# Loading wo, gate and up in whole transfers and projecting after all heads, in a one-token transformer block

## Chip, cores, metric

One NeuronCore of one Trainium2 chip. The metric is device time in microseconds (us); most executions agree within 0.3%. The span of a profile is about 2 us shorter than the time of a run.

## The reference

One token (S = 1, D = 640) goes through attention over the last W = 1024 positions of a K/V cache with 32 heads of 128, and a gated feed-forward part with F = 1728. Everything is bf16.

```python
h  = x + A(layernorm(x))      # q = x@wq; softmax(q k^T / sqrt(128)) v over the last 1024 positions; @wo
h2 = h + B(layernorm(h))      # (gelu(x@w_gate) * (x@w_up)) @ w_down
```

There is next to no reuse: 33.9 MB of cache and weights are read once. A *run* below is a stretch of bytes that lie together both in DRAM and in a partition of SBUF; a *packet* is one record of a DMA engine in the trace, and here a run is one packet.

## The kernel before

All loads are issued from one queue, in order: x, wq (2), K (16), V (8) with a quarter of wo behind every second V, gate and up in two column halves, wd (5). The parts that matter here:

```python
ones_f32 = const.tile([P, P], fp32, name="ones_f32")
one11_bf = const.tile([1, 1], bf16, name="one11_bf")
...
x_row = work.tile([1, D], bf16, name="x_row")
...
wo_src = A_wo.rearrange("(h d) n -> d h n", d=Dh)          # runs of 640 x 2 B
for c in range(NGV):
    vnat = vpool.tile([P, GV, NS, Dh], bf16, name="vnat")
    q.dma_start(out=vnat[...], in_=A_v_cache[...].rearrange("g (p t) d -> p g t d", t=NS))   # runs of 2048 B
    if c % 2 == 1:
        q.dma_start(out=wo_sb[:, woc*8:(woc+1)*8, :], in_=wo_src[:, woc*8:(woc+1)*8, :])
for (b0, b1) in cg_bounds:                                   # 2 column halves
    q.dma_start(out=wgu_sb[:, 0, :, c0:c1], in_=wg_src[:, :, c0:c1])
    q.dma_start(out=wgu_sb[:, 1, :, c0:c1], in_=wu_src[:, :, c0:c1])
...                                                          # wd in 5 transfers
for h in range(Hq):
    emit_pv(h)                                               # 8 matmuls and a cast
    if h % 8 == 4 and h // 8 >= 1:
        emit_oproj_group(h // 8 - 1)                         # 40 matmuls between V tiles
emit_oproj_group(3)
...                                                          # LayerNorm
for (b0, b1) in cg_bounds:                                   # gate and up of a half, gelu of that half
    ...
for kt in range(NFT):                                        # down: 70 matmuls
    ...
```

Of the kernel before, what the change touches and what calls it, by code (L numbers as in the profile page):

```python
# [9 lines left out]
ALU = mybir.AluOpType  # L10
ACT = mybir.ActivationFunctionType
AX = mybir.AxisListType
# [3 lines left out]
def kernel(  # L16
# [13 lines left out]
    nc = tc.nc  # L30
    bf16 = mybir.dt.bfloat16
    fp32 = mybir.dt.float32
    P = 128

    D = A_x.shape[-1]
    KT = D // P
    Dh = 128
    Hq = A_wq.shape[1] // Dh
# [6 lines left out]
    F = B_w_gate.shape[1]  # L45
    NFT = (F + P - 1) // P
# [9 lines left out]
    q = nc.sync  # L56

    const = ctx.enter_context(tc.tile_pool(name="const", bufs=1))
    wpool = ctx.enter_context(tc.tile_pool(name="wpool", bufs=1))
    work = ctx.enter_context(tc.tile_pool(name="work", bufs=1))  # L60
# [5 lines left out]
    ident_bf = const.tile([P, P], bf16, name="ident_bf")  # L66
    make_identity(nc, ident_bf[:])
    ones_f32 = const.tile([P, P], fp32, name="ones_f32")
    nc.vector.memset(ones_f32[:], 1.0)
    one11_bf = const.tile([1, 1], bf16, name="one11_bf")  # L70
    nc.vector.memset(one11_bf[:], 1.0)
    eps_t = const.tile([P, 1], fp32, name="eps_t")
    nc.vector.memset(eps_t[:], eps)

    x_row = work.tile([1, D], bf16, name="x_row")
    q.dma_start(out=x_row[:], in_=A_x.rearrange("b s d -> (b s) d"))  # L76

    wq_sb = wpool.tile([P, KT, Hq * Dh], bf16, name="wq_sb", tag="wA")
    wo_sb = wpool.tile([P, Hq, D], bf16, name="wo_sb", tag="wA")
    wgu_sb = wpool.tile([P, 2, KT, F], bf16, name="wgu_sb", tag="wF")  # L80
    wd_sb = wpool.tile([P, NFT, D], bf16, name="wd_sb", tag="wD")

# [6 lines left out]
    for c in range(NG):  # L89
        knat = kpool.tile([P, G, NS, Dh], bf16, name="knat")  # L90
        q.dma_start(  # L91
            out=knat[:, :, :, :],
            in_=A_k_cache[0, c * G : (c + 1) * G, S0:Sk, :].rearrange("g (p t) d -> p g t d", t=NS),
        )
        k_tiles.append(knat)
    wo_src = A_wo.rearrange("(h d) n -> d h n", d=Dh)
    WOCH = 8
    v_tiles = []
    for c in range(NGV):
        vnat = vpool.tile([P, GV, NS, Dh], bf16, name="vnat")  # L100
        q.dma_start(  # L101
            out=vnat[:, :, :, :],
            in_=A_v_cache[0, c * GV : (c + 1) * GV, S0:Sk, :].rearrange("g (p t) d -> p g t d", t=NS),
        )
        v_tiles.append(vnat)
        if c % 2 == 1:
            woc = c // 2
            q.dma_start(out=wo_sb[:, woc * WOCH : (woc + 1) * WOCH, :], in_=wo_src[:, woc * WOCH : (woc + 1) * WOCH, :])  # L108
    wg_src = B_w_gate.rearrange("(kt p) n -> p kt n", p=P)
    wu_src = B_w_up.rearrange("(kt p) n -> p kt n", p=P)  # L110
    NCG = 2
    cg_bounds = []
    b = 0
    for i in range(NCG):
        e = b + (NFT - b + (NCG - i) - 1) // (NCG - i)
        cg_bounds.append((b, e))
        b = e
    for (b0, b1) in cg_bounds:
        c0, c1 = b0 * P, min(b1 * P, F)
        q.dma_start(out=wgu_sb[:, 0, :, c0:c1], in_=wg_src[:, :, c0:c1])  # L120
        q.dma_start(out=wgu_sb[:, 1, :, c0:c1], in_=wu_src[:, :, c0:c1])  # L121
    nfull = NFT - 1
    wd_full_src = B_w_down[0 : nfull * P, :].rearrange("(kt p) n -> p kt n", p=P)
    NWD = 4
    b = 0
    for i in range(NWD):
        e = b + (nfull - b + (NWD - i) - 1) // (NWD - i)
        q.dma_start(out=wd_sb[:, b:e, :], in_=wd_full_src[:, b:e, :])  # L128
        b = e
# [3 lines left out]
    for c in range(KT):  # L133
        nc.tensor.matmul(
            xcol_ps[:, c : c + 1],
            lhsT=x_row[0:1, c * P : (c + 1) * P],
            rhs=one11_bf[0:1, 0:1],
            start=True,
            stop=True,
        )  # L140
    stats1 = work.tile([P, 2 * KT], fp32, name="stats1")
    nc.vector.tensor_copy(out=stats1[:, 0:KT], in_=xcol_ps[:, 0:KT])
    nc.vector.tensor_tensor(
        out=stats1[:, KT : 2 * KT], in0=stats1[:, 0:KT], in1=stats1[:, 0:KT], op=ALU.mult
# [7 lines left out]
    def ln_stats(bsum_ps, tagp):  # L152
# [24 lines left out]
        out=xn_col[:, :],  # L177
        in0=stats1[:, 0:KT],
        scalar1=mean1[:, 0:1],
        scalar2=rstd1[:, 0:1],  # L180
        op0=ALU.subtract,
        op1=ALU.mult,
# [4 lines left out]
    for h in range(Hq):  # L187
        for kt in range(KT):
            nc.tensor.matmul(  # L189
                q_ps[:, h : h + 1],  # L190
                lhsT=wq_sb[:, kt, h * Dh : (h + 1) * Dh],
                rhs=xn_col[:, kt : kt + 1],
                start=(kt == 0),
                stop=(kt == KT - 1),
# [48 lines left out]
    for t in range(NS):  # L243
        nc.tensor.transpose(
            out=srow_ps[0:Hq, t * P : (t + 1) * P],
            in_=sc_sb[:, t, :],
# [9 lines left out]
        out=e_sb[:, :],  # L256
        in_=srow_ps[0:Hq, :],
        func=ACT.Exp,
        bias=nbias[:, 0:1],
        scale=sm_scale,  # L260
# [7 lines left out]
    for t in range(NS):  # L268
        nc.tensor.transpose(
            out=eT_ps[:, t, :],  # L270
            in_=e_sb[0:Hq, t * P : (t + 1) * P],
# [7 lines left out]
    att2 = att2_ctx.enter_context(tc.tile_pool(name="att2", bufs=1, space=bass.MemoryType.PSUM))  # L279
    NOB = 4  # L280
    o_ps = att2.tile([P, NOB, 512], fp32, name="o_ps")
    o_sb = work.tile([P, Hq], bf16, name="o_sb")
    HG = 8
    NHG = Hq // HG
    opart_ps = att2.tile([P, NHG, KT], fp32, name="opart_ps")

    def emit_pv(h):
        vnat = v_tiles[(h // rep) // GV]
        g = (h // rep) % GV
        ocol = o_ps[:, h % NOB, (h // NOB) : (h // NOB) + 1]  # L290
        for t in range(NS):
            nc.tensor.matmul(  # L292
                ocol,
                lhsT=vnat[:, g, t, :],
                rhs=eT_sb[:, t, h : h + 1],
                start=(t == 0),
                stop=(t == NS - 1),
            )
        nc.vector.tensor_copy(out=o_sb[:, h : h + 1], in_=ocol)  # L299

    def emit_oproj_group(hg):
        for n in range(KT):
            for j in range(HG):
                h = hg * HG + j
                nc.tensor.matmul(  # L305
                    opart_ps[:, hg, n : n + 1],
                    lhsT=wo_sb[:, h, n * P : (n + 1) * P],
                    rhs=o_sb[:, h : h + 1],
                    start=(j == 0),
                    stop=(j == HG - 1),  # L310
                )

    for h in range(Hq):
        emit_pv(h)
        if h % HG == HG // 2 and h // HG >= 1:
            emit_oproj_group(h // HG - 1)
    emit_oproj_group(NHG - 1)
    attn_col = work.tile([P, KT], fp32, name="attn_col")
    nc.vector.tensor_reduce(
        out=attn_col[:, :],  # L320
        in_=opart_ps[:, :, :].rearrange("p g n -> p n g"),
        axis=AX.X,
        op=ALU.add,
    )

    h_col = work.tile([P, KT], fp32, name="h_col")
    nc.vector.tensor_tensor(out=h_col[:, :], in0=stats1[:, 0:KT], in1=attn_col[:, :], op=ALU.add)
    att2_ctx.close()
    stats2 = work.tile([P, 2 * KT], fp32, name="stats2")
    nc.vector.tensor_copy(out=stats2[:, 0:KT], in_=h_col[:, :])  # L330
# [3 lines left out]
    mean2, rstd2 = ln_stats(bsum2_ps, "ln2")  # L334
    hn_col = work.tile([P, KT], bf16, name="hn_col")
    nc.vector.tensor_scalar(
        out=hn_col[:, :], in0=h_col[:, :], scalar1=mean2[:, 0:1], scalar2=None, op0=ALU.subtract
# [3 lines left out]
    gu_ps = ffn_psum.tile([P, 2, NFT], fp32, name="gu_ps")  # L341
    nc.vector.memset(gu_ps[:, :, :], 0.0)
    down5 = ffn_psum.tile([P, KT, 512], fp32, name="down5")
    rsh = work.tile([P, 1], fp32, name="rsh")
    nc.vector.tensor_scalar_mul(out=rsh[:, :], in0=rstd2[:, 0:1], scalar1=0.5)
    g_sb = work.tile([P, NFT], fp32, name="g_sb")
    t1 = work.tile([P, NFT], fp32, name="t1")
    t2 = work.tile([P, NFT], fp32, name="t2")
    th = work.tile([P, NFT], fp32, name="th")
    gh = work.tile([P, NFT], fp32, name="gh")  # L350
    a_sb = work.tile([P, NFT], bf16, name="a_sb")
    for (b0, b1) in cg_bounds:
        for nt in range(b0, b1):
            M = P if nt < NFT - 1 else FT_LAST
            for which in range(2):
                for kt in range(KT):
                    nc.tensor.matmul(  # L357
                        gu_ps[0:M, which, nt : nt + 1],
                        lhsT=wgu_sb[:, which, kt, nt * P : nt * P + M],
                        rhs=hn_col[:, kt : kt + 1],  # L360
                        start=(kt == 0),
                        stop=(kt == KT - 1),
                    )
        sl = slice(b0, b1)
        nc.vector.tensor_scalar_mul(out=g_sb[:, sl], in0=gu_ps[:, 0, sl], scalar1=rstd2[:, 0:1])  # L365
        nc.vector.tensor_tensor(out=t1[:, sl], in0=g_sb[:, sl], in1=g_sb[:, sl], op=ALU.mult)
        nc.vector.tensor_scalar(
            out=t1[:, sl], in0=t1[:, sl], scalar1=0.044715, scalar2=1.0, op0=ALU.mult, op1=ALU.add
        )
        nc.vector.tensor_tensor(out=t2[:, sl], in0=t1[:, sl], in1=g_sb[:, sl], op=ALU.mult)  # L370
        nc.scalar.activation(out=th[:, sl], in_=t2[:, sl], func=ACT.Tanh, scale=0.7978845608028654)
        nc.vector.scalar_tensor_tensor(
            out=gh[:, sl], in0=th[:, sl], scalar=1.0, in1=g_sb[:, sl], op0=ALU.add, op1=ALU.mult
        )
        nc.vector.scalar_tensor_tensor(
            out=a_sb[:, sl], in0=gu_ps[:, 1, sl], scalar=rsh[:, 0:1], in1=gh[:, sl], op0=ALU.mult, op1=ALU.mult
        )
    for kt in range(NFT):
        K = P if kt < NFT - 1 else FT_LAST
        for n in range(KT):  # L380
            nc.tensor.matmul(  # L381
                down5[:, n, 0:1],
                lhsT=wd_sb[0:K, kt, n * P : (n + 1) * P],
# [41 lines left out]
```

## Time and profile before

| | before |
|---|---|
| time, median of the first 5 runs | 100.46 us (100.18 to 101.45) |
| span of the profile | 98.4 us |
| queue of loads, share of 16 engines | 94.7% |
| busiest compute engine (TensorE) | 58% |

The page, its row of slices and the stretches are read in the prediction below. Two further lines of the profile before: the first, from the page, counts the packets of the DMA engines. The second is the table of stretches for 18 to 34 us, where only K is loaded (start and end, length, busy time of the five engines, granted clock, DMA share, GB/s). The DMA share is the summed time of the packets over that of 16 engines; it can pass 1, because packets overlap a little.

```profile
DMA packets 18503, 34.08 MB, mean 346 GB/s; under 512 B 635, under 2 KB 9020, under 8 KB 18492
```

```profile
18.00:34.00 16.00, 15.36 (x335) 15.05 (x336) 7.42 (x12) 5.06 (x5) 0.00 (x0) 0.77 1.05 385
```

### The profile page before, as it was taken

The page shows a single profiled execution, that of the slowest core. Times are in us where ns is not written, and L with a number is a line of the kernel's source. Part 1 is how long each engine was busy: PE and PEld are TensorE (multiplying, and loading weights), DVE is VectorE, ACT ScalarE, POOL GpSimd, SP SyncE. Part 2 cuts the span into 40 slices and gives each one's busy share as a digit, 9 for nine tenths or more (in the row PEclk, how much of TensorE's full clock was granted, in tenths as well). Part 3 has the DMA queues.
Part 4 walks back from the last instruction along what each step waited for, and adds up shares of the span by engine and source line. Part 5 has one row for each costly group of instructions (what it writes and reads, how often), then busy time and mean ns, then how long its engine had stood idle before and what let it go on. Part 6 is the DMA issues. An engine that isn't in the chain of part 4 may idle for free.

```text
span 98.4 us, 3010 instructions
## 1 busy us (share of the span) xinstructions
PE 57.4 (58%) x1380; PEld 54.1 (55%) x1380; DVE 27.3 (28%) x95; ACT 18.9 (19%) x23; POOL 0.7 (1%) x6
## 2 busy tenths in 40 slices
PE   1791790699999999996129259044441511618650
PEld 0790790699989898985119259034331501618540
DVE  1310000035465556564535023020220320210400
ACT  5240000004436272544280000000000070000000
POOL 2000000000000000000000000000000000000000
PEclk9999855555899999999955555555555555555555
DMA  1899999999999999999999999999999999999400
GB/s 14 300 381 390 419 423 392 387 386 383 384 386 385 382 387 384 386 381 361 381 387 372 363 382 385 367 373 386 377 366 375 383 378 375 378 371 355 164 17 1
DMA packets 18503, 34.08 MB, mean 346 GB/s; under 512 B 635, under 2 KB 9020, under 8 KB 18492
## 3 DMA queue, kind: packets, MB, share of 16 engines
q1 hardware_dynamic: 18492, 33.90, 94.7%
q8 instruction: 10, 0.16, 0.7%
q14 instruction: 1, 0.01, 0.0%
HBM read 33.90 MB, written 0.00 MB: 344 GB/s over the span
## 4 chain that ended last, share of the span: by engine, by line
SPq 54%; DMA 27%; PE 14%; issue 1%; DVE 1%; DVEq 0%
SPq L101 23%; DMA wq_sb<-in_A_wq_dram 17%; DMA wd_sb<-in_B_w_down_dram 10%; SPq L108 9%; PE kT_ps L213 8%; SPq L120 7%; SPq L128 7%; SPq L121 7%; PE q_ps L189 2%; PE sc_ps L226 2%; PE down L381 1%; DVE kT_sb L218 1%; SPq L87 0%; SPq L91 0%; SPq L76 0%
## 5 line engine op out<-in xcount | busy, mean ns | idle before, releaser
L213 PE MATMUL kT_ps<-ident_bf,knat 128*128 128x128 bf16 x256 | 18.8, 234 | 0.0
L216 ACT COPY kT_sb<-kT_ps 128x1024 bf16<-128x1024 bf16 x11 | 11.1, 1012 | 28.5 <-PE kT_ps L213 28.5
L218 DVE COPY kT_sb<-kT_ps 128x1024 bf16<-128x1024 bf16 x21 | 13.7, 687 | 10.5 <-PE kT_ps L213 10.5
L213 PEld LDWEIGHTS <-knat 128*128 128x128 bf16 x256 | 16.4, 106 | 0.0
L292 PE MATMUL o_ps<-eT_sb,vnat 128*128 128x1 bf16 x256 | 7.9, 165 | 9.3 <-issue 5.6
L292 PEld LDWEIGHTS <-vnat 128*128 128x128 bf16 x256 | 7.4, 104 | 9.7 <-issue 6.3
L226 PE MATMUL sc_ps<-q_sb,kT_sb 128*128 128x1 bf16 x256 | 10.0, 164 | 1.4 <-DVE kT_sb L218 0.9
L226 PEld LDWEIGHTS <-kT_sb 128*128 128x128 bf16 x256 | 8.8, 97 | 2.1 <-DVE kT_sb L218 1.3
L299 DVE CAST o_sb<-o_ps 128x1 bf16<-128x1 f32 x32 | 5.2, 161 | 17.0 <-PE o_ps L292 15.7
L357 PE MATMUL gu_ps<-hn_col,wgu_sb 128*128 128x1 bf16 (+1 forms) x140 | 4.7, 168 | 8.1 <-DMA wgu_sb<-in_B_w_up_dram 4.6
L357 PEld LDWEIGHTS <-wgu_sb 128*128 128x128 bf16 (+1 forms) x140 | 4.5, 108 | 8.3 <-DMA wgu_sb<-in_B_w_up_dram 4.8
L189 PE MATMUL q_ps<-xn_col,wq_sb 128*128 128x1 bf16 x160 | 4.5, 165 | 6.1 <-DMA wq_sb<-in_A_wq_dram 6.1
L189 PEld LDWEIGHTS <-wq_sb 128*128 128x128 bf16 x160 | 4.3, 102 | 6.6 <-DMA wq_sb<-in_A_wq_dram 6.6
L305 PE MATMUL opart_ps<-o_sb,wo_sb 128*128 128x1 bf16 x160 | 5.2, 165 | 4.3 <-DMA wo_sb<-in_A_wo_dram 4.2
L305 PEld LDWEIGHTS <-wo_sb 128*128 128x128 bf16 x160 | 4.8, 104 | 4.6 <-DMA wo_sb<-in_A_wo_dram 4.4
L169 ACT ACTIVATE lnv_ln<-var_ln,eps_t 128x1 f32<-128x1 f32 x2 | 0.6, 294 | 30.3 <-DVE var_ln L165 30.3
L150 PEld LDWEIGHTS <-ident_bf 128*128 128x128 bf16 x36 | 4.0, 150 | 0.3 <-issue 0.3
L150 PE MATMUL junk_ps<-ident_bf 128*128 128x128 bf16 x36 | 4.0, 310 | 0.3 <-DVE tot_ln L154 0.3
L200 DVE CAST q_sb<-q_ps 128x32 bf16<-128x32 f32 x1 | 0.2, 192 | 14.1 <-PE q_ps L189 14.1
L381 PE MATMUL down<-a_sb,wd_sb 128*128 128x1 bf16 (+1 forms) x70 | 2.6, 166 | 1.7 <-DMA wd_sb<-in_B_w_down_dram 1.7
L381 PEld LDWEIGHTS <-wd_sb 128*128 128x128 bf16 (+1 forms) x70 | 2.3, 105 | 2.0 <-DMA wd_sb<-in_B_w_down_dram 2.0
L365 DVE TENSOR_SCALAR g_sb<-gu_ps,rstd_ln 128x7 f32<-128x7 f32 x2 | 0.5, 226 | 8.5 <-PE gu_ps L357 8.5
(56 smaller groups left out, 25.4 us busy)
## 6 DMA issues: line engine op xcount, KB each, us to landing
knat<-in_A_k_cache_dram SPq DMA_DIRECT2D x16, 512.0 KB, 10.8
vnat<-in_A_v_cache_dram SPq DMA_DIRECT2D x8, 1024.0 KB, 13.5
wq_sb<-in_A_wq_dram SPq DMA_DIRECT2D x2, 2560.0 KB, 13.0
wo_sb<-in_A_wo_dram SPq DMA_DIRECT2D x4, 1280.0 KB, 14.4
wd_sb<-in_B_w_down_dram SPq DMA_DIRECT2D x3, 480.0 KB, 10.3
wgu_sb<-in_B_w_gate_dram SPq DMA_DIRECT2D x1, 1120.0 KB, 16.8
wgu_sb<-in_B_w_up_dram SPq DMA_DIRECT2D x1, 1120.0 KB
wgu_sb<-in_B_w_gate_dram SPq DMA_DIRECT2D x1, 1040.0 KB, 15.4
```

The costliest lines, as they stand in the source:

```text
L101: q.dma_start(out=vnat[:, :, :, :], in_=A_v_cache[0, c * GV : (c + 1) * GV, S0:Sk, :].rearrange("g (p t) d -> p g t d", t=NS),)
L108: q.dma_start(out=wo_sb[:, woc * WOCH : (woc + 1) * WOCH, :], in_=wo_src[:, woc * WOCH : (woc + 1) * WOCH, :])
L120: q.dma_start(out=wgu_sb[:, 0, :, c0:c1], in_=wg_src[:, :, c0:c1])
L150: nc.tensor.matmul(junk_ps[:, :], lhsT=ident_bf[:, :], rhs=ident_bf[:, :], start=True, stop=True)
L189: nc.tensor.matmul(q_ps[:, h : h + 1], lhsT=wq_sb[:, kt, h * Dh : (h + 1) * Dh], rhs=xn_col[:, kt : kt + 1], start=(kt == 0), stop=(kt == ...
L213: nc.tensor.transpose(out=kT_ps[:, t, :], in_=knat[:, g, t, :], identity=ident_bf[:, :])
L216: nc.scalar.copy(out=kT_sb[:, :, :], in_=kT_ps[:, :, :])
L218: nc.vector.tensor_copy(out=kT_sb[:, :, :], in_=kT_ps[:, :, :])
L226: nc.tensor.matmul(sc_ps[:, t, h : h + 1], lhsT=kT_sb[:, t, :], rhs=q_sb[:, h : h + 1], start=True, stop=True,)
L292: nc.tensor.matmul(ocol, lhsT=vnat[:, g, t, :], rhs=eT_sb[:, t, h : h + 1], start=(t == 0), stop=(t == NS - 1),)
L305: nc.tensor.matmul(opart_ps[:, hg, n : n + 1], lhsT=wo_sb[:, h, n * P : (n + 1) * P], rhs=o_sb[:, h : h + 1], start=(j == 0), stop=(j == H ...
L357: nc.tensor.matmul(gu_ps[0:M, which, nt : nt + 1], lhsT=wgu_sb[:, which, kt, nt * P : nt * P + M], rhs=hn_col[:, kt : kt + 1], start=(kt = ...
```

## The change

The intent: fewer and longer runs in the loads, and one projection after all heads instead of four groups. wo is viewed so that a partition holds 32 neighbouring rows; o must then be permuted to match, which a 32x32 block transpose and a matmul with a permutation do.

```diff
+    perm_bf = const.tile([P, P], bf16, name="perm_bf")
+    nc.vector.tensor_copy(out=perm_bf ... "p (h a)", in_=ident_bf ... "p (a h)")
+    padc = const.tile([P, 32], bf16, name="padc")
+    nc.vector.memset(padc[:], 0.0)
...
+    pad = work.tile([P, 64], bf16, name="pad")
+    nc.vector.memset(pad[:], 0.0)
     x_row = work.tile([1, D], bf16, name="x_row")
...
-    wo_src = A_wo.rearrange("(h d) n -> d h n", d=Dh)
+    wo_src = A_wo.rearrange("(p r) n -> p (r n)", p=P)
+    q.dma_start(out=wo_sb[:, :, :].rearrange("p r n -> p (r n)"), in_=wo_src)     # ahead of V
     for c in range(NGV):
...
-        if c % 2 == 1:
-            q.dma_start(out=wo_sb[:, woc * WOCH : ...], in_=wo_src[...])
...
-    for (b0, b1) in cg_bounds:
-        q.dma_start(out=wgu_sb[:, 0, :, c0:c1], in_=wg_src[:, :, c0:c1])
-        q.dma_start(out=wgu_sb[:, 1, :, c0:c1], in_=wu_src[:, :, c0:c1])
+    q.dma_start(out=wgu_sb[:, 0, :, :], in_=wg_src[:, :, :])
+    q.dma_start(out=wgu_sb[:, 1, :, :], in_=wu_src[:, :, :])
...
-    (o projection in 4 groups of 40 matmuls between the heads, and a sum of the groups)
+    nc.vector.transpose(out=o_blk[:, :], in_=o_sb[:, :])
+    nc.tensor.matmul(perm_ps[:, :], lhsT=perm_bf[:, :], rhs=o_blk[:, :], start=True, stop=True)
+    nc.vector.tensor_copy(out=o_perm[:, :], in_=perm_ps[:, :])
+    (160 matmuls of wo_sb[:, r, ...] with o_perm[:, r])
...
-    (gate, up and gelu in two column halves)
+    (all of gate, all of up, then gelu once)
```

More of the change, by code (lines that the diff above doesn't have):

```diff
@@ L69 @@
     nc.vector.memset(ones_f32[:], 1.0)
+    perm_bf = const.tile([P, P], bf16, name="perm_bf")
+    nc.vector.tensor_copy(
+        out=perm_bf[:, :].rearrange("p (h a) -> p h a", a=4),
+        in_=ident_bf[:, :].rearrange("p (a h) -> p h a", a=4),
+    )
+    padc = const.tile([P, 32], bf16, name="padc")
+    nc.vector.memset(padc[:], 0.0)
     one11_bf = const.tile([1, 1], bf16, name="one11_bf")
@@ L78 @@
     wq_sb = wpool.tile([P, KT, Hq * Dh], bf16, name="wq_sb", tag="wA")
-    wo_sb = wpool.tile([P, Hq, D], bf16, name="wo_sb", tag="wA")
+    DJ = Dh // 32
+    RWO = (Hq * Dh) // P
+    wo_sb = wpool.tile([P, RWO, D], bf16, name="wo_sb", tag="wA")
     wgu_sb = wpool.tile([P, 2, KT, F], bf16, name="wgu_sb", tag="wF")
@@ L95 @@
         k_tiles.append(knat)
-    wo_src = A_wo.rearrange("(h d) n -> d h n", d=Dh)
-    WOCH = 8
+    wo_src = A_wo.rearrange("(p r) n -> p (r n)", p=P)
+    q.dma_start(out=wo_sb[:, :, :].rearrange("p r n -> p (r n)"), in_=wo_src)
     v_tiles = []
@@ L105 @@
         v_tiles.append(vnat)
-        if c % 2 == 1:
-            woc = c // 2
-            q.dma_start(out=wo_sb[:, woc * WOCH : (woc + 1) * WOCH, :], in_=wo_src[:, woc * WOCH : (woc + 1) * WOCH, :])
     wg_src = B_w_gate.rearrange("(kt p) n -> p kt n", p=P)
     wu_src = B_w_up.rearrange("(kt p) n -> p kt n", p=P)
-    NCG = 2
-    cg_bounds = []
-    b = 0
-    for i in range(NCG):
-        e = b + (NFT - b + (NCG - i) - 1) // (NCG - i)
-        cg_bounds.append((b, e))
-        b = e
-    for (b0, b1) in cg_bounds:
-        c0, c1 = b0 * P, min(b1 * P, F)
-        q.dma_start(out=wgu_sb[:, 0, :, c0:c1], in_=wg_src[:, :, c0:c1])
-        q.dma_start(out=wgu_sb[:, 1, :, c0:c1], in_=wu_src[:, :, c0:c1])
+    q.dma_start(out=wgu_sb[:, 0, :, :], in_=wg_src[:, :, :])
+    q.dma_start(out=wgu_sb[:, 1, :, :], in_=wu_src[:, :, :])
     nfull = NFT - 1
@@ L282 @@
     o_sb = work.tile([P, Hq], bf16, name="o_sb")
-    HG = 8
-    NHG = Hq // HG
-    opart_ps = att2.tile([P, NHG, KT], fp32, name="opart_ps")
-    def emit_pv(h):
+    for h in range(Hq):
         vnat = v_tiles[(h // rep) // GV]
@@ L299, in emit_pv @@
         nc.vector.tensor_copy(out=o_sb[:, h : h + 1], in_=ocol)
-    def emit_oproj_group(hg):
-        for n in range(KT):
-            for j in range(HG):
-                h = hg * HG + j
-                nc.tensor.matmul(
-                    opart_ps[:, hg, n : n + 1],
-                    lhsT=wo_sb[:, h, n * P : (n + 1) * P],
-                    rhs=o_sb[:, h : h + 1],
-                    start=(j == 0),
-                    stop=(j == HG - 1),
-                )
-    for h in range(Hq):
-        emit_pv(h)
-        if h % HG == HG // 2 and h // HG >= 1:
-            emit_oproj_group(h // HG - 1)
-    emit_oproj_group(NHG - 1)
-    attn_col = work.tile([P, KT], fp32, name="attn_col")
-    nc.vector.tensor_reduce(
-        out=attn_col[:, :],
-        in_=opart_ps[:, :, :].rearrange("p g n -> p n g"),
-        axis=AX.X,
-        op=ALU.add,
-    )
+    o_perm = work.tile([P, 32], bf16, name="o_perm")
+    o_blk = work.tile([P, 32], bf16, name="o_blk")
+    nc.vector.transpose(out=o_blk[:, :], in_=o_sb[:, :])
+    perm_ps = att2.tile([P, 32], fp32, name="perm_ps")
+    nc.tensor.matmul(
+        perm_ps[:, :],
+        lhsT=perm_bf[:, :],
+        rhs=o_blk[:, :],
+        start=True,
+        stop=True,
+    )
+    nc.vector.tensor_copy(out=o_perm[:, :], in_=perm_ps[:, :])
+    attn_ps = att2.tile([P, KT], fp32, name="attn_ps")
+    for n in range(KT):
+        for r in range(RWO):
+            nc.tensor.matmul(
+                attn_ps[:, n : n + 1],
+                lhsT=wo_sb[:, r, n * P : (n + 1) * P],
+                rhs=o_perm[:, r : r + 1],
+                start=(r == 0),
+                stop=(r == RWO - 1),
+            )
     h_col = work.tile([P, KT], fp32, name="h_col")
-    nc.vector.tensor_tensor(out=h_col[:, :], in0=stats1[:, 0:KT], in1=attn_col[:, :], op=ALU.add)
+    nc.vector.tensor_tensor(out=h_col[:, :], in0=stats1[:, 0:KT], in1=attn_ps[:, :], op=ALU.add)
     att2_ctx.close()
@@ L351 @@
     a_sb = work.tile([P, NFT], bf16, name="a_sb")
-    for (b0, b1) in cg_bounds:
-        for nt in range(b0, b1):
+    for which in range(2):
+        for nt in range(NFT):
             M = P if nt < NFT - 1 else FT_LAST
-            for which in range(2):
-                for kt in range(KT):
-                    nc.tensor.matmul(
-                        gu_ps[0:M, which, nt : nt + 1],
-                        lhsT=wgu_sb[:, which, kt, nt * P : nt * P + M],
-                        rhs=hn_col[:, kt : kt + 1],
-                        start=(kt == 0),
-                        stop=(kt == KT - 1),
-                    )
-        sl = slice(b0, b1)
-        nc.vector.tensor_scalar_mul(out=g_sb[:, sl], in0=gu_ps[:, 0, sl], scalar1=rstd2[:, 0:1])
-        nc.vector.tensor_tensor(out=t1[:, sl], in0=g_sb[:, sl], in1=g_sb[:, sl], op=ALU.mult)
-        nc.vector.tensor_scalar(
-            out=t1[:, sl], in0=t1[:, sl], scalar1=0.044715, scalar2=1.0, op0=ALU.mult, op1=ALU.add
-        )
-        nc.vector.tensor_tensor(out=t2[:, sl], in0=t1[:, sl], in1=g_sb[:, sl], op=ALU.mult)
-        nc.scalar.activation(out=th[:, sl], in_=t2[:, sl], func=ACT.Tanh, scale=0.7978845608028654)
-        nc.vector.scalar_tensor_tensor(
-            out=gh[:, sl], in0=th[:, sl], scalar=1.0, in1=g_sb[:, sl], op0=ALU.add, op1=ALU.mult
-        )
-        nc.vector.scalar_tensor_tensor(
-            out=a_sb[:, sl], in0=gu_ps[:, 1, sl], scalar=rsh[:, 0:1], in1=gh[:, sl], op0=ALU.mult, op1=ALU.mult
-        )
@@ new lines @@
+            for kt in range(KT):
+                nc.tensor.matmul(
+                    gu_ps[0:M, which, nt : nt + 1],
+                    lhsT=wgu_sb[:, which, kt, nt * P : nt * P + M],
+                    rhs=hn_col[:, kt : kt + 1],
+                    start=(kt == 0),
+                    stop=(kt == KT - 1),
+                )
+    sl = slice(0, NFT)
+    nc.vector.tensor_scalar_mul(out=g_sb[:, sl], in0=gu_ps[:, 0, sl], scalar1=rstd2[:, 0:1])
+    nc.vector.tensor_tensor(out=t1[:, sl], in0=g_sb[:, sl], in1=g_sb[:, sl], op=ALU.mult)
@@ new lines @@
+    nc.vector.tensor_scalar(
+        out=t1[:, sl], in0=t1[:, sl], scalar1=0.044715, scalar2=1.0, op0=ALU.mult, op1=ALU.add
+    )
+    nc.vector.tensor_tensor(out=t2[:, sl], in0=t1[:, sl], in1=g_sb[:, sl], op=ALU.mult)
+    nc.scalar.activation(out=th[:, sl], in_=t2[:, sl], func=ACT.Tanh, scale=0.7978845608028654)
+    nc.vector.scalar_tensor_tensor(
+        out=gh[:, sl], in0=th[:, sl], scalar=1.0, in1=g_sb[:, sl], op0=ALU.add, op1=ALU.mult
+    )
+    nc.vector.scalar_tensor_tensor(
+        out=a_sb[:, sl], in0=gu_ps[:, 1, sl], scalar=rsh[:, 0:1], in1=gh[:, sl], op0=ALU.mult, op1=ALU.mult
+    )
```

## The prediction

> **What bounds the kernel now.** I read the page from the top: busy shares, the row of slices, the chain that ended last, the transfers, then the timeline of the last 25 us and the table of stretches.
>
> The slices first. The three rows are the TensorE clock in tenths, the busy share of the DMA engines and their GB/s, 2.46 us to a digit:
>
> ```profile
> PE 57.4 (58%) x1380; PEld 54.1 (55%) x1380; DVE 27.3 (28%) x95; ACT 18.9 (19%) x23; POOL 0.7 (1%) x6
> ...
> PEclk9999855555899999999955555555555555555555
> DMA  1899999999999999999999999999999999999400
> GB/s 14 300 381 390 419 423 392 387 386 383 384 386 385 382 387 384 386 381 361 381 387 372 363 382 385 367 373 386 377 366 375 383 378 375 378 371 355 164 17 1
> ```
>
> No compute engine is busy over 58%, while the DMA row is at 9 from slice 2 to slice 36. So the kernel is one stream of 33.9 MB, and its end is the end of the stream plus what is computed after it. The chain agrees: it is made of the queue's issues[...] and of two transfers.
>
> ```profile
> SPq 54%; DMA 27%; PE 14%; issue 1%; DVE 1%; DVEq 0%
> ```
>
> The timeline of the end shows what stands behind the last byte:
>
> ```profile
> 94.72 0.70 PEld L381 LDWEIGHTS <-wd_sb 128*128 128x128 bf16 x20 [0.83 <-DMA wd_sb<-in_B_w_down_dram]
> 94.73 0.79 PE L381 MATMUL down<-a_sb,wd_sb 128*128 128x1 bf16 x20 [0.74 <-DMA wd_sb<-in_B_w_down_dram]
> ...
> 96.31 0.30 SPq L394 DMA_DIRECT2D out_dram<-outT_sb  x1
> ```
>
> The last piece of wd lands at 94.7 us; the other 3.7 us of the 98.4 us span are 20 matmuls, an add, a transpose, a copy and the store, which the change leaves alone.
>
> Last, the rate of the stream by stretch. In each row the last two numbers are the DMA share and GB/s. The stretches are wq alone, K, V mixed with wo, gate and up, and wd:
>
> ```profile
> 4.00:15.00 11.00, 8.07 (x135) 7.54 (x133) 0.48 (x3) 1.78 (x3) 0.00 (x0) 0.85 1.02 405
> 18.00:40.00 22.00, 21.13 (x464) 20.67 (x465) 10.81 (x18) 8.10 (x8) 0.00 (x0) 0.83 1.05 385
> 55.00:75.00 20.00, 8.01 (x264) 7.54 (x264) 3.77 (x24) 0.00 (x0) 0.00 (x0) 0.50 1.06 375
> 78.00:88.00 10.00, 2.94 (x77) 2.69 (x77) 1.96 (x12) 1.99 (x4) 0.00 (x0) 0.50 1.06 376
> 89.00:91.00 2.00, 1.98 (x63) 1.97 (x64) 0.00 (x0) 0.00 (x0) 0.00 (x0) 0.50 1.05 357
> ```
>
> The engines are fully busy in all five, yet move 405, 385, 375, 376 and 357 GB/s. The runs that lie together in DRAM, read off the kernel's slices, are 4096 B (wq), 2048 B (K and V), 1280 B (wo, wd) and 1792 or 1664 B (gate, up). The rate falls with the run.
>
> **What the skill says.** The Trainium skill, "DMA: Bandwidth & Descriptors", section "Why small descriptors are slow", states a fixed cost per packet and per descriptor. The five stretches agree in kind. With 16 engines, 4096 B at 405 GB/s take 161.8 ns and 2048 B at 385 take 85.1 ns; the line through both is 0.03745 ns per byte and 8.4 ns per run. Checked on stretches that it was not drawn from: 1280 B gives 56.3 ns, 364 GB/s (measured 357), and 1728 B, the middle of gate and up, 73.1 ns, 378 (measured 376). The same page, "Where 436 GB/s comes from", puts the ceiling at 435 GB/s; the line's own limit for an endless run is 427, and the trace never holds above 423 for a slice. "HBM Reference", section "Specifications (TRN2)", gives 358 GB/s for each core of a pair but says that one alone goes well above it; this trace, at 405, agrees with the second. Last, "VectorE: DVE Perf Modes", section "The three transpose paths", says that VectorE transposes 32x32 blocks only, which is why the change needs a permuting matmul behind it; the trace before has none.
>
> **The change, part by part.**
>
> *wo as one transfer.* Rows are now grouped by 32 to a partition, so that the run is 32 x 640 x 2 = 40,960 B instead of 1280. 5.243 MB at 364 GB/s are 14.4 us. If a run stays one descriptor, 40,960 B take 1542 ns, 425 GB/s, and the whole 12.3 us: 2.1 us saved. If it is cut at 4096 B, the rate is wq's 405 and the transfer 12.95 us: 1.5 us saved.
>
> *Gate and up as one transfer each.* The run becomes 3456 B: 137.8 ns, 401 GB/s. 4.424 MB go from 11.7 us at 378 to 11.0: 0.7 us saved.
>
> *The order.* wo moves in front of V. The sum of bytes is the same, [...]wq's readers, whose buffer wo takes, are done at 20.5 us while the last K issue is at 31.4. No gap in the stream is to be expected.
>
> So the last landing moves up by 2.2 to 2.8 us, if nothing takes its place.
>
> *The compute added and moved.* Before, three of four groups of output projection ran in waits between V tiles; now all 160 matmuls stand behind the last V. Counted from the landing of the last V tile, with durations from the timeline before (TensorE at half clock): the last four heads 1.0 us and a cast 0.2; block transpose, permuting matmul and copy about 0.8 together (three dependent instructions like others of 0.2 to 0.3); 160 projection matmuls at 1.23 us per 40, 4.9; then h_col to hn_col, in the trace from 77.39 to 79.20, 1.8, and 0.2 for a semaphore or two: 8.9. Gate's 70 matmuls at 1.90 per 65 take 2.05: 10.95. Up lands 11.0 behind V, so its 70 matmuls end near 13.1; the chain from g_sb to a_sb was 1.5 (85.30 to 86.84): 14.6; the first 50 down matmuls, 20 in 0.69, 1.7: 16.3. The last of wd lands 11.0 + 2.21 MB / 364 GB/s = 17.1 behind V. So TensorE gets to the last piece of wd about 0.8 us before it lands, and the last landing still sets the end. This slack is smaller than before, when a_sb was done at 92.84, 1.8 us ahead of the last landing. Nothing of this adds time unless the slack is used up.
>
> The added set-up (two memsets and a strided copy of the identity, well under 1 us on VectorE) lies ahead of a wq that lands at 10.5 us. It costs nothing.
>
> Sum: 100.46 - 2.5 = 97.9 us, 2.5% faster.
>
> **The rivals.**
>
> First, the long runs bring nothing over 2048 B, because memory itself gives 385 here or because 16 engines, each deep in one row, meet in the same memory banks. For it: the rate in wq's own stretch wavers between 373 and 434 from one us to the next. Against it: the mean there is 405. wo then saves 14.4 - 13.6 = 0.8 and gate and up 0.2 to 0.7: 99.0 to 99.5 us, within 2%.
>
> Second, the serial chain behind the last V becomes the bound: a projection without overlap, at half clock, with LayerNorm, gate, up and gelu behind it. For it: the slack above is only 0.8 us, and my figure for the three new instructions is an estimate. Against it: the wait for up and the wait for wd absorb what comes early. If the chain is 1.5 us longer than I make it, 0.7 us of the gain is lost: 98.6 us, just within 2%.
>
> Third, a wait moves into the stream: wo in front of V sits in the queue until wq's buffer is free. The times above (20.5 against 31.4 us) speak against it. It would show as a dip in the GB/s row, and cost its length; I give it little.
>
> Fourth, more than I think: if the stream's engines end more evenly (the row falls off over 91 to 94 us: 148 GB/s in that stretch) or runs of 40 KB reach the ceiling, 3.2 us are saved: 97.2 us.
>
> **Range and chances.** The mechanism, fewer and longer runs in a stream that is the bound, is seen in five stretches of one trace; what isn't seen is any run over 4096 B, and that is the larger half of the gain. The 2% line is at 98.45 us, a saving of 2.0. wo at 405 with gate and up at 401 just passes it (2.2), wo at 425 passes it well (2.8); the first and second rival fall short. I put the first at about one in five, a shortfall through the second or through mixed small losses at a little over one in ten, and a loss of more than 2% at almost nothing, since nothing adds bytes. The range is 96.7 to 99.3.
>
> **What would show it.** Right: a GB/s row over 400 for about 12 us after K, near 385 for V, near 400 for gate and up; fewer packets by 4,100 to 5,200 (wo from 4096 to 128 or 1280, gate and up from 2560 to 1280); the last 20 down matmuls still waiting for wd; the last landing near 92.2 us in the span. The chain wrong: those matmuls run without a wait for a transfer, and the chain of what ended last goes back over the projection to the last V. The rate wrong: about 385 GB/s or less while wo is loaded. The whole would be wrong if the stream showed a slice below 9 between 10 and 85 us.

## More of the kernel before

Tiles are laid out in SBUF in the order in which they and their pools are declared: const, weights, work, kT, K, V. A tile declared early moves the address of all that come later.

## The result

| | before | after |
|---|---|---|
| time, median | 100.45 us (16 runs) | 94.36 us (94.10 to 94.60, 9 runs) |
| ratio of times | | 0.939 (0.937 to 0.941) |
| span of the profile | 98.4 us | 92.4 us |

A ratio here is the mean time of one kernel's fast runs over that of the other's fast runs of the same rounds, so it is not quite the ratio of the medians quoted beside it. The kernel is 6.1 us faster. I had said 2.5, with a range of 1.2 to 3.8: the direction was right and the size was wrong, outside the range.

The rows of slices of the profile after (2.31 us to a digit):

```profile
DMA  0899999999999999897978999999999999999300
GB/s 13 282 376 381 408 422 411 405 407 414 394 409 404 401 409 579 349 532 326 514 321 344 407 405 406 411 409 407 400 411 419 422 411 419 406 386 383 144 7 1
DMA packets 13175, 34.08 MB, mean 369 GB/s; under 512 B 555, under 2 KB 2284, under 8 KB 13036
```

The packets fell by 5,328: 5,248 of wo, gate and up, just past the upper end of what was foretold (wo stays in runs of 40,960 B), and 80 of 4 B. While wo is loaded (36.4 to 50.3 us, slices 15 to 21), the GB/s row swings between 321 and 579 and the DMA row falls to 7 and 8. By the prediction's last sign, a slice below 9, that would be a gap in the stream. It is none: the profile books a packet's bytes and time wholly where it starts, and these packets last 1.5 us. Spread over each packet's own time, the same records give 431 GB/s at a share of 1.00 from 40 to 48 us.

What was not foretold stands to the left of that. The same stretch of K as above, in the kernel after:

```profile
18.00:34.00 16.00, 15.43 (x342) 15.12 (x342) 7.42 (x12) 5.10 (x6) 0.00 (x0) 0.79 1.05 405
```

The last number went from 385 to 405 GB/s. In this stretch both kernels load the same K tiles, in the same order, with the same runs of 2048 B, and wo, gate and up have not begun. Long runs in later transfers cannot do this. And V, which I had left at "near 385", runs at 406:

```profile
60.00:68.00 8.00, 3.04 (x96) 2.80 (x96) 1.93 (x12) 0.00 (x0) 0.00 (x0) 0.50 1.05 406
```

The end of TensorE's timeline after (start, length, what ran, and in brackets the idle time before it and what ended it):

```profile
83.28 2.25 PE L348 MATMUL gu_ps<-hn_col,wgu_sb 128*128 128x1 bf16 x70 [0.30 <-DMA wgu_sb<-in_B_w_up_dram]
87.19 2.11 PE L372 MATMUL down<-a_sb,wd_sb 128*128 128x1 bf16 x70 [1.67 <-DVE a_sb L366]
```

Before, the last 20 down matmuls waited for wd. Now all 70 run in one piece behind a_sb, so the work behind the landing of up has become as long as what remained of the stream: the last packet of wd ended at 88.40 us, about 0.3 before TensorE came to its last 20 matmuls.

I also read the single packets in the records of the traces: mean ns of one packet, by its size. The two right columns are experiments told below.

| packet | before | after | old code, starts aligned | new code, old starts |
|---|---|---|---|---|
| 1280 B | 60.0 | 55.0 | 55.2 | 59.0 |
| 1664 / 1792 B | 74.8 / 78.7 | | 69.0 / 74.4 | |
| 2048 B | 88.4 | 84.3 | 84.4 | 88.3 |
| 3456 B | | 135.8 | | 140.8 |
| 40,960 B | | 1522 | | 1524 |

A packet of 1280 or 2048 B was 4 to 5 ns shorter after. What differs for K and V is where they land. From the layout of the two programs: before, K and V tiles start 224 bytes behind a multiple of 256 in a partition and all weights 192 behind one; after, all of them start at a multiple of 256. For the weights the 64 bytes of `padc` do that (the new constant has 256, which changes nothing here); for K and V these 64, the 128 of `pad`, and 96 by which the other small tiles of the change grew.

### The profile page after: what moved, and what is told of

Read it like the earlier page. It is cut to its first block, busy times and chain, and to the rows that moved or that the text cites. A ratio compares the mean times of both kernels' runs of the same rounds, so it can differ in the third digit from the quotient of the medians.

```text
span 92.4 us, 3004 instructions
## 1 busy us (share of the span) xinstructions
PE 56.9 (62%) x1381; PEld 53.7 (58%) x1381; DVE 26.6 (29%) x93; ACT 18.7 (20%) x22; POOL 0.7 (1%) x6
## 4 chain that ended last, share of the span: by engine, by line
DMA 40%; SPq 35%; PE 18%; DVE 3%; issue 1%; ACT 0%; DVEq 0%
SPq L112 30%; DMA wgu_sb<-in_B_w_up_dram 22%; DMA wq_sb<-in_A_wq_dram 18%; PE kT_ps L212 8%; SPq L119 3%; PE q_ps L188 2%; PE gu_ps L348 2%; PE down L372 2%; PE sc_ps L225 2%; DVE kT_sb L217 1%; SPq L108 0%; SPq L98 0%; SPq L102 0%; SPq L85 0%; PE outT_ps L382 0%
## 5 line engine op out<-in xcount | busy, mean ns | idle before, releaser
L287 PE MATMUL o_ps<-eT_sb,vnat 128*128 128x1 bf16 x256 | 8.1, 166 | 13.5 <-DMA vnat<-in_A_v_cache_dram 13.5
L310 PE MATMUL attn_ps<-o_perm,wo_sb 128*128 128x1 bf16 x160 | 4.6, 165 | 1.2 <-issue 0.9
L372 PE MATMUL down<-a_sb,wd_sb 128*128 128x1 bf16 (+1 forms) x70 | 2.1, 165 | 1.7 <-DVE a_sb L366 1.7
```

Of the source, the lines that this page charges most:

```text
L287: nc.tensor.matmul(ocol, lhsT=vnat[:, g, t, :], rhs=eT_sb[:, t, h : h + 1], start=(t == 0), stop=(t == NS - 1),)
L310: nc.tensor.matmul(attn_ps[:, n : n + 1], lhsT=wo_sb[:, r, n * P : (n + 1) * P], rhs=o_perm[:, r : r + 1], start=(r == 0), stop=(r == RWO ...
L372: nc.tensor.matmul(down5[:, n, 0:1], lhsT=wd_sb[0:K, kt, n * P : (n + 1) * P], rhs=a_sb[0:K, kt : kt + 1], start=(kt == 0), stop=(kt == NF ...
```

## The experiments

**Theory A**: the start address of a destination in its partition, relative to 256 bytes, sets the time of a packet; most of the surprise is that. **Theory B**: the long runs, the order and the late projection make the whole gain, K's rate included, in some way that I don't see.

### 1. The old code with aligned starts

```diff
+    padc = const.tile([P, 32], bf16, name="padc")     # and a memset
+    pad = work.tile([P, 240], bf16, name="pad")       # and a memset
```

> The kernel before with nothing changed but two unused tiles (64 and 480 bytes) ahead of the others, so that K and V tiles start at the SBUF addresses of the changed kernel (a multiple of 512) and all weights at multiples of 256. Theory A (start addresses of the destinations set the rate of the stream): the K stretch (18 to 40 us) goes from 385 to 408 GB/s or more, and the time falls by 2.6 us for K and V (16.8 MB) and by 1 to 2 us for the weights, to 96 to 97 us. Theory B (all of the gain is in the long runs and the new order): 100.4 us, K at 385. Theory C (the gain comes from a chip or run difference): before and this kernel agree.

Measured: 95.59 us against 100.48, ratio 0.949 (0.941 to 0.956). Its K stretch:

```profile
18.00:34.00 16.00, 15.54 (x347) 15.23 (x348) 7.42 (x12) 5.32 (x6) 0.00 (x0) 0.80 1.05 405
```

Two unread tiles bring 4.9 us, a little more than Theory A expected (to 96; its 408 GB/s for K was a little high), with no load, run, order or other computation changed. Theory B has fallen; so has a difference of chip or day, since both kernels ran in the same rounds.

### 2. The new code at the old starts

```diff
-    padc = const.tile([P, 32], bf16, name="padc")
-    pad = work.tile([P, 64], bf16, name="pad")
+    pad = work.tile([P, 80], bf16, name="pad")
```

> The changed kernel with its two pad tiles taken out and one of 160 bytes put in, so that K and V start 224 bytes behind a multiple of 256 and the weights 192 bytes behind one, as in the kernel before. Long runs, order and the late projection stay. Theory A: K back at 385 GB/s, time 97.3 to 98.0 us, near the 97.9 of the prediction, whose working left addresses out. Theory B: 94.4 us as with the pads.

Measured: 97.63 us, ratio 0.969 (0.963 to 0.976). Its K stretch:

```profile
18.00:34.00 16.00, 15.37 (x346) 15.06 (x347) 7.42 (x12) 5.30 (x6) 0.00 (x0) 0.82 1.05 385
```

K is back at 385. This is the kernel whose time my working had worked out, 97.9 us: long runs, order and late projection bring 2.85 us at unchanged starts. Here the last 20 down matmuls (14 and 6) still wait for wd, as foretold:

```profile
91.69 0.53 PE L370 MATMUL down<-a_sb,wd_sb 128*128 128x1 bf16 x14 [0.37 <-DMA wd_sb<-in_B_w_down_dram]
```

### 3 and 4. Weights alone, K and V alone

Both are the old code. The first has pads of 64 and 448 bytes (weights aligned, K and V still 224 off), the second one of 32 bytes (K and V aligned, weights still 192 off).

> The kernel before with pads of 64 and 448 bytes: the weights start at multiples of 256, K and V still 224 behind one. Theory A: K at 385 GB/s, the wd stretch better than 357, time 98.5 to 99.5 us. Theory B: 100.4 us.

> The kernel before with one pad of 32 bytes: K and V start at multiples of 512, the weights stay 192 behind a multiple of 256. Theory A: K at 408 GB/s or more, time 97.5 to 98.2 us. Theory B: 100.4 us. If the effects are additive, the gains of this run and of the one with aligned weights sum to that of the run with both.

Measured: 97.35 us, ratio 0.968 (0.961 to 0.976), with K at 387; and 97.83 us, ratio 0.972 (0.965 to 0.980), with K at 405. Each half does its part. The weights bring more than I expected (3.1 us against at most 1.9). The two gains sum to 5.8 us, while both together gave 4.9. The intervals of the times are about 0.8 us to either side, but the spans of the same runs scatter by 0.3 us at most and say the same: 2.9 and 2.7 us, against 4.6 together. The traces point to where the gains overlap: the stretch in which V is mixed with wo (55 to 70 us) ran at 377 GB/s before, at 395 and 397 in these two, and at 400 in experiment 1. Aligning either half brings most of the gain there; experiment 14 meets the same.

### 5 and 6. How far off is off

The new code with `pad` of 192 and of 256 bytes instead of 128: K and V start 64 and 128 bytes behind a multiple of 256, the weights stay aligned.

> The changed kernel with its 128-byte pad made 192 bytes: K and V start 64 bytes behind a multiple of 256, the weights stay at multiples of 256. Theory A1 (any start off a multiple of 256 costs): K stretch (18 to 34 us) at 385 instead of 405 GB/s, time 94.4 + 2.6 = 97.0 us. Theory A2 (only starts off a multiple of 64 cost for K and V): 405 GB/s and 94.4 us.

> As the run before with 256 bytes of pad: K and V start 128 bytes behind a multiple of 256. Theory A1: 385 GB/s, 97.0 us. Theory A3 (what counts is a multiple of 128): 405 GB/s, 94.4 us.

Measured: 96.51 us, ratio 0.960 (0.953 to 0.967), and 96.44 us, ratio 0.959 (0.953 to 0.965), some 2.1 us over the kernel after. The K stretches, 64 bytes off first:

```profile
18.00:34.00 16.00, 15.40 (x354) 15.10 (x355) 7.36 (x13) 5.56 (x6) 0.00 (x0) 1.00 1.05 388
```

```profile
18.00:34.00 16.00, 15.54 (x357) 15.23 (x358) 7.52 (x13) 5.73 (x6) 0.00 (x0) 1.00 1.05 388
```

Multiples of 64 or of 128 don't do: both lose nearly as much as 224 bytes off (385). The granted clock was 1.00 here against 0.8 in the runs above; that does not set the rate (experiment 13: 405 GB/s at a clock of 1.00, the kernel after: 405 at 0.79).

The Trainium skill, "DMA: Bandwidth & Descriptors", section "How a descriptor splits into AXI transactions", has the like: a descriptor is moved in transactions of 256 B, and one that starts off a multiple of 256 begins with one at the boundary below. A run of 2048 B then takes nine instead of eight. I had this section in reach when I predicted and did not apply it. It agrees with these runs in the size of 256. What it says of the cost is tested in experiments 13 to 18.

### 7 and 8. What is left for the long runs once starts are aligned

7 is the new code with gate and up in column halves again, in transfers and computation. 8 is the old code with aligned starts and with gate and up merged, so it differs from the kernel after in wo and its projection alone.

> The changed kernel with gate and up cut in two column halves again, in their transfers and in the computation (runs of 1792 and 1664 B), destinations at multiples of 256. Theory A with a stream at its limit: 1280 runs of 3456 B at 135 ns become 1280 pairs of 74 and 69 ns, 80 runs an engine, 8 ns each: 0.6 us more, 95.0 us. Rival (the merge pays nothing once starts are on multiples of 256, or the shorter work behind the last landing makes up for it): 94.2 to 94.5 us.

> The kernel before with starts aligned and gate and up merged: wo still in runs of 1280 B in four transfers between V tiles, projection in four groups between V tiles. If the gains of the long runs are additive in the stream, gate and up bring 0.6 us against the aligned kernel before (95.6): 95.0 us, and wo's long run the remaining 0.6 to the changed kernel. If wo's late projection costs what its long run brings, this one is at 94.4 or below.

Measured: 94.55 us, ratio 0.941 (0.935 to 0.946), and 95.33 us, ratio 0.949 (0.943 to 0.956). Against the kernel after (0.939), splitting gate and up costs about 0.2 us, within the noise, and wo in short runs, with its projection in groups, about 1.0. So with aligned starts the merge of gate and up pays nearly nothing and wo's part about 1 us; my expectation of 0.6 for each was wrong in the split, not in the sum.

### 9. The order

The wo transfer is moved behind the V loop.

```diff
-    q.dma_start(out=wo_sb..., in_=wo_src)     # ahead of V
+    q.dma_start(out=wo_sb..., in_=wo_src)     # behind V
```

> The changed kernel with the one wo transfer issued behind V instead of ahead of it; same bytes, runs and addresses. If the order has no part in the gain (the stream is the bound and has no gap): 94.1 to 94.7 us. If wo ahead of V is what helps (K and V drawn apart): 95 us or more. If the work behind the last V counts: a little under 94.4, since the last heads are then done when wo lands.

Measured: 94.17 us, ratio 0.938 (0.934 to 0.942). The order has no part in the gain.

### 10. Is the work behind up the bound now?

```diff
-    gu_ps = ffn_psum.tile([P, 2, NFT], fp32, name="gu_ps")
+    g_ps = psum_a.tile([P, NFT], fp32, name="g_ps", tag="m2")
+    u_ps = ffn_psum.tile([P, NFT], fp32, name="u_ps")
     (gate's matmuls into g_ps, the steps from g_sb to gh, then up's matmuls into u_ps, then a_sb)
```

> The changed kernel with gate's sums in a PSUM tile of their own, so that the five steps from g_sb to gh run beside up's matmuls; only a_sb is left behind up: 1.4 us less serial work after up lands. If the stream is the bound again: 94.2 to 94.4 us. If the chain from up's landing is the bound: up to 1 us less, 93.4 us.

Measured: 94.34 us, ratio 0.939 (0.935 to 0.943). The end of its TensorE timeline:

```profile
85.74 1.07 PE L385 MATMUL down<-a_sb,wd_sb 128*128 128x1 bf16 x35 [0.32 <-DVE a_sb L379]
...
88.67 0.79 PE L385 MATMUL down<-a_sb,wd_sb 128*128 128x1 bf16 x20 [0.94 <-DMA wd_sb<-in_B_w_down_dram]
```

The down matmuls start 1.4 us sooner, and then the last 20 wait again for wd, until 88.67; they end at 89.46, where the kernel after ended its own at 89.30. So in the kernel after, stream and chain end together. The late projection has used up the slack, but it has cost nothing yet.

### 11 and 12. A longer run for wd

wd's first 1664 rows are grouped by 13 to a partition, in four transfers as before (runs of 5120 and 3840 B), and the columns of gate and up are taken with a step of 13 to match. 12 adds the edit of experiment 10.

```diff
-    wd_full_src = B_w_down[0 : nfull * P, :].rearrange("(kt p) n -> p kt n", p=P)
+    wd_full_src = B_w_down[0 : nfull * P, :].rearrange("(p kt) n -> p kt n", p=P)
...
-    lhsT=wgu_sb[:, which, kt, nt * P : nt * P + M],
+    lhsT=wgu_sb[:, which, kt, nt : nfull * P : nfull]     # the last block as before
```

> The changed kernel with wd's first 1664 rows grouped by 13 to a partition: runs of 5120 and 3840 B instead of 1280 B, gate's and up's weight columns taken with a step of 13 so that the rows match. Stream: 1664 packets of 55 ns become 512 of about 150 to 195 ns, 0.4 to 0.5 us less. If the stream is the bound: 93.9 us. If the chain from up's landing is: 94.4 us, or more if the stepped weight loads are slow.

> The two runs before together. If each alone brings little because stream and chain end together, the two together bring 0.4 to 0.6 us: 93.8 us. If the stepped weight loads are slow (more than 0.031 us a matmul), nothing or a loss.

Measured: 97.87 us, ratio 0.975 (0.970 to 0.979), and 96.62 us, ratio 0.962 (0.958 to 0.967): slower than the kernel after by 3.5 and 2.3 us. TensorE's line for gate and up in experiment 11:

```profile
80.49 8.73 PE L348 MATMUL gu_ps<-hn_col,wgu_sb 128*128 128x1 bf16 x140 [0.87 <-DVE var_ln L164]
```

140 matmuls take 8.73 us, 62 ns each, where the 70 of up in the kernel after took 2.25 us, 32 ns each. With a stepped column a matmul here takes twice as long (the weight loads alone took 161 ns each against 104), and this chain, now 4 us longer, is the bound. The gain of wd's longer runs stays open: a layout that needs no stepped load was not tried. No version that loads everything beat the kernel after by more than noise.

### 13 to 18. Which property of the start costs

Theory A in its simple form (each start off 256 costs) has a flaw. Rows of gate and up lie 3456 B apart, 13.5 times 256, so half of their runs start 128 bytes off in the aligned kernels too; yet in experiment 7 each of their 1280 packets of 1792 B took 74 ns. And K and V had always been at multiples of 512 where they were fast. 13 puts them at odd multiples of 256. 14 leaves 128 bytes between the two heads of a K tile, so that half of K's runs are 128 off. 15 and 16 load only 1792 of each 2048 B of K, at 0 and at 128 bytes off; 17 and 18 do so with 1920 B.

```diff
# 13: pad of 384 bytes.   14: knat tile of 2112 elements, heads 1088 elements apart, one transfer a head
# 15 to 18 (not the reference's computation; 16 and 18 with a pad of 256 bytes):
-    out=knat[:, :, :, :],   in_=... "g (p t) d -> p g t d"
+    out=knat[:, :, 0:7, :], in_=... "g (p t) d -> p g t d" [:, :, 0:7, :]                     # 15, 16
+    out=knat (t d joined) [:, :, 0:960], in_=... "g (p t) d -> p g (t d)" [:, :, 0:960]       # 17, 18
-    nc.tensor.transpose(..., in_=knat[:, g, t, :], ...)
+    nc.tensor.transpose(..., in_=knat[:, g, min(t, 6), :], ...)                               # 15 to 18
```

> The changed kernel with a pad of 384 bytes: K and V start at odd multiples of 256 instead of multiples of 512. If 256 is the unit: K stretch 405 GB/s, 94.4 us. If 512 is: 388 GB/s and 96.5 us.

> The changed kernel with 128 bytes between the two heads of a K tile, loaded by one transfer a head, so that half of K's runs start at a multiple of 256 and half 128 behind one; V at odd multiples of 256. If each run off 256 pays by itself: half of K's packets of 2048 B at 84 ns, the rest slower, K stretch near 396 GB/s. If a run 128 off is free among others, as it looks for gate and up: 405. If a part of them slows all: 388.

> Wrong result on purpose: of each K run of 2048 B only the first 1792 B are loaded, the last rows are read twice. K at multiples of 512. All packets of 1792 B at 74 ns. The control for the next run.

> Wrong result on purpose: as the run before, K and V 128 bytes behind a multiple of 256. If the start alone decides: the packets of 1792 B of K jitter up to 86 ns, mean near 78, K stretch 4% lower than in the control. If the length decides, or the runs of gate and up are spared because of their length: 74 ns, as in the control.

Measured: 13 took 94.38 us, ratio 0.940 (0.938 to 0.943), K at 405, so 256 is the unit, not 512:

```profile
18.00:34.00 16.00, 15.49 (x354) 15.18 (x355) 7.41 (x13) 5.56 (x6) 0.00 (x0) 1.00 1.05 405
```

14, 15 and 16 had one look each (94.56, 91.78 and 94.10 us), and only K's stretch is read of them. The stretches of 14, of 15 and of 16:

```profile
18.00:34.00 16.00, 15.69 (x347) 14.92 (x348) 7.52 (x12) 5.18 (x6) 0.00 (x0) 0.83 1.05 400
```

```profile
18.00:34.00 16.00, 15.84 (x353) 15.71 (x354) 7.67 (x13) 5.69 (x6) 0.00 (x0) 0.77 1.05 400
```

```profile
18.00:34.00 16.00, 15.80 (x360) 15.67 (x361) 8.05 (x13) 6.07 (x6) 0.00 (x0) 0.81 1.06 383
```

In 14 nearly every packet of K took 84 ns, those 128 off as well: a run off 256 is free, or nearly (400 GB/s against 405), if its neighbours are not off. In 16, where all are, 1792 B lose like 2048. So neither the single start nor the length decides. What fits is a second limit beside the first. Suppose that on the SBUF side a run takes one slot for each window of 256 bytes that it touches, full or not, at the 435 GB/s of the prediction's page (wo's long packets came to 431 above): then the stream moves at 435 x bytes / (256 x windows) GB/s, or at the limit seen with aligned starts, about 405 for such runs, whichever is lower. A run of 1920 B at 128 off ends on a boundary and touches eight windows, as many as at 0. The last two runs were made for that:

> Wrong result on purpose: of each K run of 2048 B only 1920 B are loaded. K at multiples of 512: eight windows of 256 are touched. All K packets alike, K stretch near 403 GB/s. The control for the next run.

> Wrong result on purpose: the same 1920 B, with all K and V starts 128 bytes behind a multiple of 256. A run now ends at a multiple of 256 and touches eight windows, as in the control. Model of slots: 435 x 1920 / 2048 = 408 GB/s is above the other limit, so K runs as in the control, packets without jitter, while V (2048 B at 128, nine slots) is at 387. Plain cost of a start off 256: K 4 to 5% under the control, as 1792 and 2048 B at 128 were (383 against 400, 388 against 405).

Measured, one look each (93.10 and 94.16 us). K in 17, then K and V in 18:

```profile
18.00:34.00 16.00, 15.43 (x344) 15.14 (x345) 7.51 (x12) 5.21 (x6) 0.00 (x0) 0.80 1.05 404
```

```profile
18.00:34.00 16.00, 15.45 (x340) 15.16 (x341) 7.52 (x12) 5.06 (x5) 0.00 (x0) 0.79 1.05 403
55.00:68.00 13.00, 5.07 (x160) 4.66 (x160) 3.23 (x20) 0.00 (x0) 0.00 (x0) 0.50 1.05 385
```

In one and the same run K, 128 bytes off, loads at full rate, because 1920 B touch no window more; V, 128 bytes off, loses, because 2048 B do. The plain cost of a start off 256 has fallen, the count of windows has passed a test it could have failed. The cases beside it (wo's by bytes spread over each packet's time):

| load (run, bytes off 256) | windows | 435 x share used, an estimate | measured GB/s |
|---|---|---|---|
| K before, 2048 at 224 | 9 | 387 | 385 |
| K in 5 and 6, 2048 at 64 and 128 | 9 | 387 | 388, 388 |
| K after, 2048 at 0 | 8 | 435 | 405 |
| K in 14, half at 0, half at 128 | 8.5 | 410 | 400 |
| K in 15 and 16, 1792 at 0 and 128 | 7, 8 | 435, 381 | 400, 383 |
| K in 17 and 18, 1920 at 0 and 128 | 8, 8 | 408, 408 | 404, 403 |
| gate and up before, 1792 and 1664 at 192 and 64 | 15.5 a row | 379 | 376 |
| V with wo, before; 3 and 4; 1 | 9 and 6; 9 and 5, 8 and 6; 8 and 5 | 377; 404, 404; 435 | 377; 395, 397; 400 |
| wd before, 1280 at 192; in 3 at 0 | 6; 5 | 363; 435 | 357; 386 (2 us only) |
| wq before, 4096 at 192; after at 0 | 17; 16 | 409; 435 | 405; 402 |
| wo after, 40,960 at 0 | 160 | 435 | 431 |

Where the estimate is under 400 it is what was measured to 2%; where it is over, the other limit holds, and that grows with the run (386 at 1280 B, 400 to 405 at 1792 to 4096, 431 at 40,960; a little under 400 for the mixtures). A rival fits all rows but one: that a run pays when it both starts and ends off 256. Every slow run does, and experiment 18's ends on a boundary. But wq's runs before do too and lose nothing that the traces show (the median packet takes 159 ns, before and after); only this row tells the two apart. Gate and up merged touch 14 windows in every row, at 0 or at 128 off, so they never pay once their tile is on a boundary.

## Why the prediction was wrong

Its steps, one by one.

- **What bounds the kernel: right.** The stream was the bound, and still is, if only just (experiment 10).
- **wo and gate and up in long runs: right at the old starts.** I took 2.2 to 2.8 us off the stream and chose 2.5; experiment 2 measured 2.85 with nothing else changed (97.63 us against my 97.9). wo's packets took 1524 ns, where I had 1542, so the first rival, that runs over 2048 B bring nothing, was wrong too.
- **The order: right.** No gap, no gain (experiment 9).
- **The work behind the last V: nearly right.** From the start of the last V's matmuls I counted 10.95 us to the end of gate and 14.6 to a_sb; in the profile after it is 11.7 (71.27 to 82.98) and 15.9. The slack of 0.8 was gone, but the last landing came when foretold, 17.1 us behind (88.40), so the second rival took nothing away.
- **"The added set-up (two memsets and a strided copy of the identity, well under 1 us on VectorE) ... costs nothing": this is the step that failed.** It is true of the time of these instructions and overlooks what they are for. Two tiles that nobody reads move every later tile. With it falls the term for K and V, "near 385 for V", and the term for wd (364 GB/s in my sums, 386 with aligned weights in experiment 3): I took the rate of a run length as given, where it was the rate of a run length at a bad start. Experiment 1 gives what this step left out by itself: 4.9 us, where I had nothing.

Why 4.9 and 2.85 make 6.1 and not 7.75: the two gains overlap, since both save windows and packets. An estimate from the packet table: wo in 4096 runs takes 4096 x 60.0 / 16 ns, 14.6 us at a DMA share of 1.05, and 13.5 with aligned starts; in 128 long ones 128 x 1522 / 16 ns, 12.2 us at the share of 1.00 found above, and there the start no longer matters (1524 and 1522 ns). So the long run saves 2.4 us off the old starts and 1.3 off aligned ones. Gate and up, at shares of 1.05 split and 1.03 merged: 11.7 to 10.9, against 10.9 to 10.5. Together 3.2 and 1.7 us, each 0.3 to 0.5 more than the measured 2.85 and the 1.2 between experiment 1 and the kernel after; why is open. Their difference, 1.5, is about the 1.65 by which the two gains overlap.

The fit in the prediction looked well tested, since the line through wq and K foretold the other stretches. But its points were taken under two limits at once: K, gate and up, and wd all sat on windows (387, 379, 363 in the table), and a straight line happens to run near them; wq alone did not. That 97.9 came so near to experiment 2 is in part luck. All were measured at starts off 256, so none could show the start as a cause. The spread of packet times might have: before, 14% of the packets of 2048 B took 95 ns or more while the shortest took 84; after, nearly all took 84.

That addresses do it is shown by on and off in both codes; that windows of 256 bytes are what counts is inferred from the table and from one run, seen once, that could have refuted it. What in the hardware takes a slot for a window is not shown by any run.

## What to carry to other kernels

In a kernel bound by its loads, look at the start address of every tile that a load fills before touching anything else, and count the windows of 256 bytes that its runs touch: two unread tiles brought 4.9 of 100 us here, more than all the rewriting (2.85 at the old starts, 1.2 at aligned ones). When a diff adds a tile that nobody reads, ask what it moves. Gains of longer runs and of aligned starts overlap, so measure each in the other's presence, and look at what work is left behind the last landing before making runs still longer.

## What the Trainium skill lacked or had wrong

- "SBUF — State Buffer", section "Operand start alignment", calls any start at a multiple of the element size legal and says that its runs timed nothing. The time: K in runs of 2048 B loads at 405 GB/s at a multiple of 256 (even or odd), and at 388, 388 and 385 GB/s at 64, 128 and 224 bytes behind one.
- "DMA: Bandwidth & Descriptors", section "How a descriptor splits into AXI transactions", tells this of bytes that are fetched, and lets the leftover at a run's end cost only the beats that it fills. Here only destinations in SBUF moved; 64 bytes off (2 beats more than 64 by its count) lost as much as 224 off (7 more), so each window seems to cost a whole one. And a run off 256 was free where it touched no window more (1920 B at 128: 403 GB/s, at 0: 404).
- The same page's rules for authors have none on where a destination starts; by these runs it was worth 4.9 of 100.5 us.
- No page gives a figure for the cost of a weight load with a stepped column: 62 ns a matmul instead of 32 at half clock, with a step of 13 bf16 elements.
